# Last transform of a long convolution: four array places of 64 rows by 32 columns instead of two of 128 by 64, with the token rows ordered to match

## The chip, the cores and the metric

The kernel runs on one core of a Trainium2 chip. The metric is the device time of one execution in microseconds. A core has TensorE (PE in the profile; its weight loads are listed apart as PEld), VectorE (DVE), ScalarE (ACT), GpSimd (POOL) and SyncE (SP). SP and POOL issue DMAs here.

## The reference, cut to what matters

x is one sequence of L = 2048 tokens with D = 448 channels. Two residual steps follow each other, each with a layer norm that is scaled and shifted by vectors computed from a condition c:

```python
x = A_u
mod = (_silu(c) @ w_mod).reshape(c.shape[0], 6, 1, -1)
h = _layernorm(x, axis=-1) * (1 + ca) + sa
x = x + ga * _A_ref(h, ...)        # S4D: long convolution over tokens
h = _layernorm(x, axis=-1) * (1 + cb) + sb
x = x + gb * _B_ref(h, ...)        # mixer: MLP over tokens
...
# _A_ref: K = 2 Re sum_n C exp(A dt pos), 256 terms per channel; y = u * K (causal, by FFT of 2L) + D_skip * u
# _B_ref: h = layernorm(x); u = gelu(h^T w1 + b1) with 1792 features; y = u w2 + b2
```

## The kernel before

The convolution is a two-step Fourier transform of length 4096, written as matmuls in fp32 with small tables. A token number is split so that one step works over 32 values (n in the code), the other over 64. The channels go in two halves of 224. The program has these stages:

- Until about 384 us: the convolution's filter is generated (exponentials and sines on ACT, products on POOL and DVE, matmuls on PE), its spectrum and that of the input are made, and the first half of the channels goes through the spectral product and the inverse transform.
- 384 to 416 us: the second half of the channels. The loop over m takes 16 pairs of frequencies in steps of two. Per pair: `pc_s2` (a forward matmul into kx, line 770), `pc_mul` (DVE makes zx and zy from kx and the input's spectrum u, line 779; POOL makes the two halves of z, lines 781 and 782), `pc_inv` (the inverse matmuls into vv, line 796) and `pc_out` (ACT copies vv to vt, SP stores it into v_d in DRAM, lines 802 and 804). `pc_inv` of a step stands behind `pc_s2` of the next step. u is loaded by SP, four buffers deep (line 739). Inside this loop SP also loads the first weights of the mixer and the first tile of x.
- From 416 us: the mixer. Its first product runs over 16 groups r of 128 tokens each (r is the token number modulo 16). For each r, SP loads vt from v_d (`ln_load`), PE does the last transform of the convolution into one PSUM tile y with the table ft (`ln_y`, line 1222), DVE adds it to x (line 1225), and a layer norm, the modulation and a second layer norm follow on ACT and DVE. The result is split into a high and a low part, h3h and h3l. `mlp1` multiplies by weights that ACT and DVE have split too (whi, wlo, lines 202 and 211): 21 matmuls for each r and each half of the 1792 features, lines 1194 to 1196. PE's order is written out by hand: y of r = t + 3 stands ahead of the 21 matmuls of r = t.
- Then gelu, the second half of the features (meanwhile the new x rows are stored into x2_d, line 1310), and the second product with w2, which adds x2_d and writes the output, lines 1328 to 1334.

The rows of a tile of 128 tokens are ordered (g, n, h): 64 partitions for each g, in which n and h alternate. Rows of x, w1 and x2_d are therefore moved by two DMAs of 64 partitions. The table ft has 128 rows (32 frequencies k, real and imaginary part, and h) and 64 columns (n, h); where row and column differ in h it is zero. One y takes two matmuls, one for each g, of 128 rows by 64 columns.

The order of PE, ACT, DVE and POOL within a stage is that of the code (manual_schedule); SP's order is partly the code's (between the lines with `first` or `last`), partly a scheduler's. A weight tile is three buffers deep as loaded, four deep as split.

Of the kernel before, what the change touches and what calls it, by code (L numbers as in the profile page):

```python
# [11 lines left out]
F32 = mybir.dt.float32  # L12
# [9 lines left out]
L, D, N, F = 2048, 448, 256, 1792  # L22
P = 128
# [16 lines left out]
def dft_tables():  # L40
    n1 = np.arange(32)
    k1 = np.arange(32)
    n2 = np.arange(64)
    k2 = np.arange(64)
    nn = 4096
    t = {}
    w = 2 * np.pi * np.outer(n1, k1) / 64
    w1 = np.zeros((2, 32, 32))
    w1[0] = np.cos(w)
    w1[1] = -np.sin(w)  # L50
    w1[0, :, 0] = 1
    w1[1, :, 0] = (-1.0) ** n1
    wc = np.zeros((4, 32, 2, 4, 32))
    for g in range(4):
        for c in range(2):
            wc[g, :, c, g, :] = w1[c]
    t["WU"] = np.tile(w1.transpose(1, 2, 0).reshape(32, 64), (4, 1))

    t["WC"] = wc.reshape(P, 2, 2, 2, 32).swapaxes(3, 4).reshape(P, 2 * P)
    s = np.zeros((2, 64, 32, 2, 64))  # L60
    i1 = np.zeros((2, 64, 32, 2, 64))
    i2 = np.zeros((2, 64, 32, 2, 64))

    def inverse(rows, cols, k, m, ang):
        a = np.cos(ang) * 2 / nn
        b = np.sin(ang) * 2 / nn
        i1[0, rows, k, m[0]] = a
        i1[1, rows, k, m[0]] = -b
        i2[1, rows, k, m[0]] = -a
        i2[0, rows, k, m[0]] = -b  # L70
        if len(m) > 1:
            i1[0, rows, k, m[1]] = b
            i1[1, rows, k, m[1]] = a
            i2[1, rows, k, m[1]] = -b
            i2[0, rows, k, m[1]] = a

    for k in range(1, 32):
        ang = 2 * np.pi * np.outer(n2, k + 64 * k2) / nn
        s[0, :, k, 0] = np.cos(ang)
        s[1, :, k, 0] = np.sin(ang)  # L80
        s[0, :, k, 1] = -np.sin(ang)
        s[1, :, k, 1] = np.cos(ang)
        inverse(slice(None), None, k, (0, 1), ang.T)


    for q in range(32):
        ang = 2 * np.pi * n2 * (32 + 64 * q) / nn
        s[1, :, 0, 0, q] = np.cos(ang)
        s[1, :, 0, 1, q] = -np.sin(ang)
        inverse(q, None, 0, (1,), ang)  # L90
    for q in range(33, 64):
        ang = 2 * np.pi * n2 * (64 * (q - 32)) / nn
        s[0, :, 0, 0, q] = np.cos(ang)
        s[0, :, 0, 1, q] = -np.sin(ang)
        inverse(q, None, 0, (0,), ang)
    s[0, :, 0, 0, 32] = 1
    s[0, :, 0, 1, 32] = (-1.0) ** n2
    i1[0, 32, 0, 0] = 1 / nn
    i2[1, 32, 0, 0] = (-1.0) ** n2 / nn
    s2 = s.reshape(P, 32 * P)  # L100

    su = s.swapaxes(3, 4).reshape(2, 64, 32, P)
    t["S2"] = su.reshape(2, 4, 8, 2, 32 * P).transpose(3, 0, 2, 1, 4).reshape(P, 32 * P)

    one = np.einsum("cnk,cqkm->km", w1, su)
    t["SV"] = one[ones_k1()].T

    order = lambda a: a.reshape(P, 32, 2, 2, 2, 16).swapaxes(3, 4).reshape(2, 64, 32, P)
    v1, v2 = order(i1), order(i2)
    pairs = v1.reshape(2, 64, NP, 2, P).transpose(3, 1, 2, 0, 4).reshape(P, NP, 2 * P)  # L110
    t["SI"] = np.concatenate([s2.reshape(P, NP, 2 * P), pairs], 2).reshape(P, NP * 4 * P)
    t0 = np.zeros((P, 2, P))
    t0[32, 0] = v1[0, 32, 0] + v2[1, 32, 0]
    t0[:, 1] = pairs[:, 0, P:]
    t["T0"] = t0.reshape(P, 2 * P)
    ft = np.zeros((32, 2, 2, 32, 2))
    w = 2 * np.pi * np.outer(k1, n1) / 64
    f0 = np.cos(w)
    f1 = -np.sin(w)
    f0[0] = 1  # L120
    f1[0] = (-1.0) ** n1
    for h in range(2):
        ft[:, 0, h, :, h] = f0
        ft[:, 1, h, :, h] = f1
    t["FT"] = ft.reshape(P, 64)


    te = np.zeros((3, 64, 16, 32))
    tg = np.zeros((3, 16, 4, 16, 32))
    n = np.arange(32)  # L130
    for d in range(16):
        te[0, 2 * d : 2 * d + 2, d] = 2 * n + 1
        te[2, 2 * d : 2 * d + 2, d] = -n
        tg[0, d, 0:2, d] = n
        tg[0, d, 2:4, d] = 1
        tg[2, d, 0:2, d] = -64 * n
        tg[2, d, 2:4, d] = 1
    tg = tg.reshape(3, 16, 2, 2, 512).swapaxes(1, 2)
    tt = np.concatenate([te.reshape(3, 64, 512), tg.reshape(3, 64, 512)], 1)
    tt[1] = -tt[0]  # L140
    t["TT"] = tt.reshape(3, P, 512)
    return {k: np.ascontiguousarray(v.astype(np.float32)) for k, v in t.items()}


def ones_k1():

    return [0] + list(range(1, 32, 2))


def token_rows(a):  # L150

    return a.rearrange("(n g h r) d -> r g n h d", g=2, h=2, r=16)


def token_pair(a, r, g):

    rows = a.rearrange("(n g h r) d -> g n h (r d)", g=2, h=2, r=16)
    return rows[g, :, :, r * D : (r + 2) * D]


class WeightStream:
# [4 lines left out]
    def __init__(self, tc, ctx, i):  # L166
        self.nc = tc.nc
        self.pool = ctx.enter_context(tc.tile_pool(name="mw", bufs=WAHEAD, side="right", reuse_waits="tile"))
        self.w1 = token_rows(i["B_w1"])
        self.w2 = i["B_w2"].rearrange("(k p) s -> p k s", p=P)  # L170
        self.raw, self.parts = {}, {}
        self.loaded = self.done = 0

    def load(self):
        n = self.loaded
        if n == 64:
            return
        w = self.pool.tile([P, 896], F32, tag="w", name="w", bufs=3)
        if n < 32:
            fh, r = divmod(n, 16)  # L180
            for g in range(2):
                self.nc.sync.dma_start(w[64 * g : 64 * g + 64], self.w1[r, g, :, :, fh * 896 : (fh + 1) * 896])
        else:
            t, kh = divmod(n - 32, 2)
            self.nc.sync.dma_start(
                w.rearrange("p (k s) -> p k s", k=7), self.w2[:, 7 * kh : 7 * kh + 7, t * P : (t + 1) * P]
            )
        self.raw[n] = w
        self.loaded += 1
# [27 lines left out]
def tile_adaln_s4d_mixer(ctx, tc, i, out):  # L217
    nc = tc.nc
    x = i["A_u"][0]
# [6 lines left out]
    v_d = dram.tile([32, P, D], F32, name="v_d")  # L226
    x2_d = dram.tile([L, D], F32, name="x2_d")

    cp = ctx.enter_context(tc.tile_pool(name="cp", bufs=1))
    mod = [None] * 3 + [cp.tile([P, D], F32, name=f"mod{k}") for k in range(3, 6)]  # L230
    eps_t = cp.tile([P, 1], F32, name="eps_t")
    ft = cp.tile([P, 64], F32, name="ft")
    b1 = cp.tile([P, 14], F32, name="b1")
    b2 = cp.tile([P, 16], F32, name="b2")
    nc.vector.memset(eps_t, EPS)
# [2 lines left out]
    with ExitStack() as es:  # L238
        V, S, G, T = nc.vector, nc.scalar, nc.gpsimd, nc.tensor
# [85 lines left out]
        for q in range(4):  # L325
            r = slice(32 * q, 32 * q + 1)
# [615 lines left out]
        rows, cols, pieces = iter(range(32)), iter(range(32)), [0, 0]  # L942
# [189 lines left out]
        xts = [xs.tile([P, 2, D], F32, name=f"xt{r}") for r in range(8)]  # L1132

        def x_pair(r):
            for g in range(2):
                nc.sync.dma_start(
                    xts[r // 2][64 * g : 64 * g + 64].rearrange("p r d -> p (r d)"), token_pair(x, r, g)
                )

        swp = es.enter_context(tc.tile_pool(name="swp", bufs=2, reuse_waits="tile"))  # L1140
# [34 lines left out]
    with ExitStack() as es:  # L1175
        es.enter_context(tc.manual_schedule(engines={ENG.PE, ENG.Activation, ENG.DVE, ENG.Pool}))
        V, S, G = nc.vector, nc.scalar, nc.gpsimd
# [4 lines left out]
        h3l = kp.tile([P, 16, D], F32R, name="h3l")  # L1182
        uh = [up.tile([P, 7, D], F32R, name="uh0"), None]
        ul = [up.tile([P, 7, D], F32R, name="ul0"), None]
        v_v = v_d.rearrange("k (ch g r) d -> r (k ch) g d", ch=4, g=2)

        def mlp1(acc, n, f0=0, f1=7):
            fh, r = divmod(n, 16)
# [9 lines left out]
        vts, hs, sa, sb = {}, {}, {}, {}  # L1198

        def ln_load(r):  # L1200
            vts[r] = rot.tile([P, 2, D], F32, tag="vt", name="vt", bufs=4)
            nc.sync.dma_start(vts[r], v_v[r])
            if r % 2 and 1 < r < 15:
                x_pair(r + 1)

        def small(nm, tag):
            return rot.tile([P, 1], F32, tag=tag + nm, name=nm, bufs=3)
# [10 lines left out]
        def ln_y(r):  # L1218
            y = py.tile([P, D], F32, tag="y", name="y")
            vt = vts.pop(r)  # L1220
            for g in range(2):
                nc.tensor.matmul(y[64 * g : 64 * g + 64], ft, vt[:, g], start=True, stop=True)  # L1222
            total = small("sum", "a")
            x_ = xts[r // 2][:, r % 2]
            V.scalar_tensor_tensor(x_, x_, 1.0, y, ALU.mult, ALU.add, accum_out=total)
            return lambda: sa.update({r: stats(x_, total, "a")})
# [78 lines left out]
        acc = [pacc.tile([P, D], F32, tag="acc", name="acc") for _ in range(7)]  # L1305
        for r in range(16):
            if r < 8:
                for g in range(2):
                    rows = xts[r][64 * g : 64 * g + 64].rearrange("p r d -> p (r d)")
                    nc.sync.dma_start(token_pair(x2_d, 2 * r, g), rows)  # L1310
            wst.ahead(16 + r + WAHEAD, V)
            mlp1(acc, 16 + r)
        e2.close()
# [3 lines left out]
        for t in range(16):  # L1317
# [4 lines left out]
            for kh in range(2):  # L1322
                n = 32 + 2 * t + kh
# [7 lines left out]
            y = ru.tile([P, D], F32, tag="y", name="y")  # L1331
# [30 lines left out]
```

## Time and profile before

| | us |
|---|---|
| median of 3 runs (719.51 to 723.74) | 723.24 |
| the profiled execution | 723.32 |
| its span | 721.5 |
| PE busy in the span | 630.4 (87%) |
| DVE busy | 453.3 (63%) |
| ACT busy | 442.9 (61%) |
| POOL busy | 273.4 (38%) |
| mean granted TensorE clock | 0.924 |

Busy times are sums over records of one execution; the ends of matmuls are modelled, and a busy PE is not a PE at its peak. Lines such as L1222 are lines of the program before. A row of the timeline is: start, length, engine, line, operation, out<-in, count, and in brackets the idle time of the engine ahead of it with what ended it. Rows with SPq are DMA issues on SP's queue: the time for which the queue was taken, not the transfer.

### The profile page before, as it was taken

The page shows a single profiled execution, that of the slowest core. Times are in us where ns is not written, and L with a number is a line of the kernel's source. Part 1 is how long each engine was busy: PE and PEld are TensorE (multiplying, and loading weights), DVE is VectorE, ACT ScalarE, POOL GpSimd, SP SyncE. Part 2 cuts the span into 40 slices and gives each one's busy share as a digit, 9 for nine tenths or more (in the row PEclk, how much of TensorE's full clock was granted, in tenths as well). Part 3 has the DMA queues.
Part 4 walks back from the last instruction along what each step waited for, and adds up shares of the span by engine and source line. Part 5 has one row for each costly group of instructions (what it writes and reads, how often), then busy time and mean ns, then how long its engine had stood idle before and what let it go on. Part 6 is the DMA issues. An engine that isn't in the chain of part 4 may idle for free. (4 is left out here: it accounts for less than half of the span.)

```text
span 721.5 us, 18291 instructions
## 1 busy us (share of the span) xinstructions
PE 630.4 (87%) x7204; PEld 455.2 (63%) x7204; DVE 453.3 (63%) x875; ACT 442.9 (61%) x879; POOL 273.4 (38%) x328
## 2 busy tenths in 40 slices
PE   0659989987899888789888949999999999999997
PEld 0334334543544546556565617778999999999996
DVE  7569779769859768476785538778723263334441
ACT  5837588777988889989983549787622242222220
POOL 6487428318729788878884600000000000000000
PEclk9869857787999999989999959999999999999999
DMA  7795464356889645535236979974585436655540
GB/s 168 203 192 139 147 198 138 114 186 164 245 250 254 183 137 131 162 86 152 71 105 184 289 221 257 243 207 112 167 233 153 143 106 176 175 156 153 154 141 25
DMA packets 101636, 121.19 MB, mean 168 GB/s; under 512 B 13067, under 2 KB 87423, under 8 KB 101423
## 3 DMA queue, kind: packets, MB, share of 16 engines
q1 hardware_dynamic: 100014, 113.16, 55.3%
q0 software_dynamic: 1536, 6.87, 4.4%
q8 instruction: 57, 0.93, 0.6%
q14 instruction: 29, 0.23, 0.1%
HBM read 84.64 MB, written 34.87 MB: 166 GB/s over the span
## 5 line engine op out<-in xcount | busy, mean ns | idle before, releaser
L202 ACT CAST whi<-w 128x896 fp32r<-128x896 f32 x64 | 59.7, 938 | 131.4 <-PE o L1329 84.6
L649 POOL TENSOR_TENSOR G<-mag,gs 128x512 f32<-128x512 f32 x56 | 71.9, 1283 | 92.4 <-ACT gs L645 92.4
L211 DVE TENSOR_TENSOR wlo<-w,whi 128x896 fp32r<-128x896 f32 x64 | 68.0, 1087 | 40.3 <-ACT whi L202 27.9
L601 PE MATMUL xg<-tab,lph 64*128 64x512 f32 x112 | 68.0, 609 | 26.6 <-issue 7.9
L1194 PE MATMUL acc<-h3h,whi 128*128 128x448 f32 x224 | 83.5, 373 | 0.1
L1195 PE MATMUL acc<-h3l,whi 128*128 128x448 f32 x224 | 82.0, 366 | 0.0
L1329 PE MATMUL o<-ul,whi 128*128 128x448 f32 x224 | 81.3, 363 | 0.0
L676 PEld LDWEIGHTS kg<-E,G 128*32 128x32 f32 x3584 | 60.7, 121 | 32.5 <-issue 19.4
L1328 PE MATMUL o<-uh,whi 128*128 128x448 f32 x224 | 81.2, 362 | 0.0
L1196 PE MATMUL acc<-h3h,wlo 128*128 128x448 f32 x224 | 81.1, 362 | 0.0
L1330 PE MATMUL o<-uh,wlo 128*128 128x448 f32 x224 | 80.6, 360 | 0.0
L601 PE MATMUL xe<-tab,lph 64*128 64x512 f32 x112 | 66.7, 599 | 12.2 <-ACT gs L646 10.0
L676 PE MATMUL kg<-E,G 128*32 128x64 f32 x3584 | 70.8, 237 | 3.1 <-issue 2.3
L650 POOL TENSOR_TENSOR G<-mag,gs 128x512 f32<-128x512 f32 x56 | 71.7, 1280 | 0.0
L651 DVE TENSOR_TENSOR E<-m,xe 128x512 f32<-128x512 f32 x56 | 38.2, 683 | 39.6 <-ACT xe L644 31.5
L630 POOL TENSOR_TENSOR m<-mag,w 128x512 f32<-128x512 f32 x56 | 59.9, 1069 | 6.0 <-DVE E L655 1.5
L1332 DVE SCALAR_TENSOR_TENSOR y<-o,b,mod 128x448 f32<-128x448 f32 x16 | 10.9, 684 | 80.3 <-PE o L1330 80.3
L642 ACT ACTIVATE ab<-xe 128x512 f32<-128x512 f32 x56 | 33.6, 600 | 31.0 <-PE xe L601 18.4
L1194 PEld LDWEIGHTS acc<-h3h,whi 128*128 128x128 f32 x224 | 42.4, 189 | 13.9 <-ACT h L1250 6.3
L601 PE MATMUL xe<-tab,lex 64*128 64x512 f32 x56 | 31.2, 567 | 19.2 <-DMA lex<-wm 17.4
L601 PEld LDWEIGHTS xg<-tab,lph 64*128 64x128 f32 x112 | 24.0, 214 | 37.1 <-issue 9.8
L612 ACT ACTIVATE mag<-xe 128x512 f32<-128x512 f32 x56 | 35.5, 634 | 17.8 <-PE xg L601 11.1
(231 smaller groups left out, 1485.9 us busy)
## 6 DMA issues: line engine op xcount, KB each, us to landing
w<-in_B_w_dram SPq DMA_DIRECT2D x64, 224.0 KB
w<-in_B_w_dram SPq DMA_DIRECT2D x32, 448.0 KB
yu_d<-yt SPq DMA_DIRECT2D x16, 448.0 KB
yi<-yu_d SPq DMA_DIRECT2D x32, 224.0 KB
us_d<-uo SPq DMA_DIRECT2D x16, 448.0 KB
u<-us_d SPq DMA_DIRECT2D x32, 224.0 KB
v_d<-vt SPq DMA_DIRECT2D x32, 224.0 KB
vt<-v_d SPq DMA_DIRECT2D x16, 448.0 KB
```

Of the source, the lines that this page charges most:

```text
L211: eng.tensor_tensor(lo, w, hi.bitcast(F32), ALU.subtract)
L601: T.matmul(out[k], lhs[r], rhs[r], start=start, stop=stop)
L630: G.tensor_tensor(m2, me, w[:, :, None].to_broadcast([P, GD, 32]), ALU.mult)
L649: G.tensor_tensor(Gt[:, 1], mg_, v32(sg), ALU.mult)
L650: G.tensor_tensor(Gt[:, 0], mg_, v32(cg_), ALU.mult)
L676: T.matmul(kgs[g][32 * q : 32 * q + 32, m], Gt[:, c, d], E[:, c, d], start=h == 0 and c == 0 and m == 0, stop=h == 1 and c == 1, skip_grou ...
L1194: nc.tensor.matmul(acc[f], hi[:, fs], h3h[:, r], start=r == 0, stop=False)
L1195: nc.tensor.matmul(acc[f], hi[:, fs], h3l[:, r], start=False, stop=False)
L1196: nc.tensor.matmul(acc[f], lo[:, fs], h3h[:, r], start=False, stop=r == 15)
L1328: nc.tensor.matmul(o, hi[:, ks], uh[kh][:, k], start=kh == 0 and k == 0, stop=False)
L1329: nc.tensor.matmul(o, hi[:, ks], ul[kh][:, k], start=False, stop=False)
L1330: nc.tensor.matmul(o, lo[:, ks], uh[kh][:, k], start=False, stop=kh == 1 and k == 6)
```

## The change

The last transform of each r is done by four matmuls of 64 rows by 32 columns, one for each pair (g, h), at array rows 64 h and array columns 32 j with j = 2 g + h. The table FT loses its zeros and has 32 columns. For this the real parts, imaginary parts and frequencies of one h have to stand in one half of the partitions, so v_d is loaded by two DMAs for each r. The token rows of a tile come out in the order (g, h, n), so every load and store of token rows (w1, x, x2_d) is four DMAs of 32 partitions instead of two of 64. The loads of x, except for the first tile, are issued on POOL's queue instead of SP's. Line numbers of the mixer move by up to 3.

```diff
-    ft = np.zeros((32, 2, 2, 32, 2))
+    ft = np.zeros((2, 32, 2, 32))
...
     for h in range(2):
-        ft[:, 0, h, :, h] = f0
-        ft[:, 1, h, :, h] = f1
-    t["FT"] = ft.reshape(P, 64)
+        ft[h, :, 0] = f0
+        ft[h, :, 1] = f1
+    t["FT"] = ft.reshape(P, 32)
...
 def token_rows(a):
-    return a.rearrange("(n g h r) d -> r g n h d", g=2, h=2, r=16)
+    return a.rearrange("(n j r) d -> r j n d", j=4, r=16)
-def token_pair(a, r, g):
-    rows = a.rearrange("(n g h r) d -> g n h (r d)", g=2, h=2, r=16)
-    return rows[g, :, :, r * D : (r + 2) * D]
+def token_pair(a, r, j):
+    rows = a.rearrange("(n j r) d -> j n (r d)", j=4, r=16)
+    return rows[j, :, r * D : (r + 2) * D]
...
-            for g in range(2):
-                self.nc.sync.dma_start(w[64 * g : 64 * g + 64], self.w1[r, g, :, :, fh * 896 : (fh + 1) * 896])
+            for j in range(4):
+                self.nc.sync.dma_start(w[32 * j : 32 * j + 32], self.w1[r, j, :, fh * 896 : (fh + 1) * 896])
...
-    ft = cp.tile([P, 64], F32, name="ft")
+    ft = cp.tile([P, 32], F32, name="ft")
...
         def x_pair(r):
-            for g in range(2):
-                nc.sync.dma_start(
-                    xts[r // 2][64 * g : 64 * g + 64].rearrange("p r d -> p (r d)"), token_pair(x, r, g)
+            for j in range(4):
+                (G if r else nc.sync).dma_start(
+                    xts[r // 2][32 * j : 32 * j + 32].rearrange("p r d -> p (r d)"), token_pair(x, r, j)
                 )
...
-        v_v = v_d.rearrange("k (ch g r) d -> r (k ch) g d", ch=4, g=2)
+        v_v = v_d.rearrange("k (c h g r) d -> r h k c g d", c=2, h=2, g=2)
...
-            nc.sync.dma_start(vts[r], v_v[r])
+            for h in range(2):
+                nc.sync.dma_start(vts[r][64 * h : 64 * h + 64], v_v[r, h])
...
-            for g in range(2):
-                nc.tensor.matmul(y[64 * g : 64 * g + 64], ft, vt[:, g], start=True, stop=True)
+            for j in range(4):
+                g, h = divmod(j, 2)
+                k = slice(64 * h, 64 * h + 64)
+                nc.tensor.matmul(y[32 * j : 32 * j + 32], ft[k], vt[k, g], start=True, stop=True)
...
-                for g in range(2):
-                    rows = xts[r][64 * g : 64 * g + 64].rearrange("p r d -> p (r d)")
-                    nc.sync.dma_start(token_pair(x2_d, 2 * r, g), rows)
+                for j in range(4):
+                    rows = xts[r][32 * j : 32 * j + 32].rearrange("p r d -> p (r d)")
+                    nc.sync.dma_start(token_pair(x2_d, 2 * r, j), rows)
```

The order of instructions on PE, DVE and ACT stays the same but for y's. On POOL and SP it changes; the places are shown in the prediction.

## The prediction

> **What bounds the kernel now.** I read the granted clock and the stretches by time first, then the chain that ended last, then the timelines of PE, POOL and SP where the edited lines run. The table of stretches gives, for each stretch, the busy time of PE, of the weight loads, of DVE, ACT and POOL (instruction counts in brackets), then the granted TensorE clock, the DMA share and GB/s.
>
> ```profile
> 424.00:432.00 8.00, 5.32 (x13) 0.88 (x9) 4.17 (x14) 2.87 (x7) 0.00 (x0) 0.50 1.06 281
> ...
> 440.00:500.00 60.00, 60.00 (x285) 46.15 (x285) 47.30 (x141) 49.29 (x108) 0.00 (x0) 1.00 0.83 204
> 500.00:590.00 90.00, 90.00 (x452) 84.36 (x451) 40.62 (x65) 34.73 (x48) 0.00 (x0) 1.00 0.54 156
> ```
>
> From 440 on PE has no gap. So whatever moves the moment at which the mixer's first accumulation starts moves the end, and so does every microsecond that PE itself spends on the last transform (tile y). The chain (start, length, engine and line) shows that moment and the pace behind it.
>
> ```profile
> 413.22 2.77 DMA v_d<-vt
> ...
> 416.39 1.27 DMA v_d<-vt
> ...
> 419.55 6.80 issue
> ...
> 431.60 0.74 PE acc L1194
> ...
> 438.47 0.20 PE acc L1195
> 438.87 0.90 PE y L1222 x4
> ...
> 444.18 0.90 PE y L1222 x4
> ```
>
> The convolution's last store leaves at 416.39, the first accumulation starts at 431.60; between them lie the stores' landing, the load of vt, one transform and one layer norm. Then one r takes 444.18 - 438.87 = 5.31 us.
>
> **The transform itself.** Now 32 matmuls of 128 rows by 64 columns become 64 of 64 rows by 32 columns. Each fp32 matmul leaves two records, so one r had 4 records and gets 8. All stream 448 columns. The first three run at half clock:
>
> ```profile
> 423.64 1.76 PE L1222 MATMUL y<-vt,ft 128*64 128x448 f32 x4 [7.94 <-DMA vt<-v_d]
> 426.13 1.76 PE L1222 MATMUL y<-vt,ft 128*64 128x448 f32 x4 [0.73 <-DVE xt L1225]
> 429.72 1.76 PE L1222 MATMUL y<-vt,ft 128*64 128x448 f32 x4 [1.83 <-DVE xt L1225]
> ```
>
> Four records in 0.90 us on the chain: already two at a time, 0.45 us for each round of 448 columns. If four go at a time, 8 records are again two rounds, 0.90 us. That four can go is seen at line 714, whose 64x64 matmuls use two row halves and two column halves:
>
> ```profile
> 382.51 1.16 PE L714 MATMUL y<-wc,ks 64*64 64x64 f32 x62 [0.22 <-ACT vt L802]
> ```
>
> At y's rate a round of 64 columns takes 0.45 x 64/448 = 0.064 us; 62 records two at a time would be 31 rounds, 2.0 us; four at a time 1.0. It took 1.16. So the change buys PE nothing: what it drops is not time but the zeros in the weights. Bounds: of the 5.31 us of one r, 21 accumulating matmuls at 0.20 (as the chain's row at 438.47) are 4.2 and y 0.90, so 0.21 is the change of form and could at best go (13 r at full clock: -2.7); four more records at L714's 1.16/62 = 0.019 us are 0.07 each r (+1.0). I take 0.
>
> **x loads on POOL.** This is the costly part. Fourteen of the sixteen x loads of 64 rows leave SP's queue and become 28 loads of 32 rows on POOL's queue, and they are not issued in the mixer but between the products of the convolution's second half.
>
> POOL in the program before, at the middle of the second half (z_6187 to z_6251 are the products' outputs of four successive spectrum pairs):
>
> ```order
> L781 TENSOR_TENSOR z_6187<-zx_6185,zy_6186 128x224
> L782 TENSOR_TENSOR z_6187<-zx_6185,zy_6186 128x224
> L781 TENSOR_TENSOR z_6197<-zx_6195,zy_6196 128x224
> L782 TENSOR_TENSOR z_6197<-zx_6195,zy_6196 128x224
> L781 TENSOR_TENSOR z_6241<-zx_6239,zy_6240 128x224
> L782 TENSOR_TENSOR z_6241<-zx_6239,zy_6240 128x224
> L781 TENSOR_TENSOR z_6251<-zx_6249,zy_6250 128x224
> L782 TENSOR_TENSOR z_6251<-zx_6249,zy_6250 128x224
> ```
>
> Nothing stands between the products. POOL in the changed program, the same four pairs ( xt2 and xt3 are x tiles of the mixer):
>
> ```order
> L1136 DMA xt2_6072<-in_A_u_dram 32x896 x2
> L781 TENSOR_TENSOR z_6187<-zx_6185,zy_6186 128x224
> L782 TENSOR_TENSOR z_6187<-zx_6185,zy_6186 128x224
> L781 TENSOR_TENSOR z_6197<-zx_6195,zy_6196 128x224
> L782 TENSOR_TENSOR z_6197<-zx_6195,zy_6196 128x224
> L1136 DMA xt2_6072<-in_A_u_dram 32x896
> L1136 DMA xt3_6073<-in_A_u_dram 32x896 x2
> L781 TENSOR_TENSOR z_6241<-zx_6239,zy_6240 128x224
> L782 TENSOR_TENSOR z_6241<-zx_6239,zy_6240 128x224
> L781 TENSOR_TENSOR z_6251<-zx_6249,zy_6250 128x224
> L782 TENSOR_TENSOR z_6251<-zx_6249,zy_6250 128x224
> L1136 DMA xt3_6073<-in_A_u_dram 32x896 x2
> ```
>
> Five loads now stand among products that followed each other directly. Number the 16 pairs of the second half z16 to z31. Over all of it, 3 loads stand ahead of z16, 21 between z16 and z31, 4 behind z31. Issuing one occupies POOL, as POOL's own earlier x loads of 32 rows show:
>
> ```profile
> L292 POOL DMA_DIRECT2D xt<-in_A_u_dram x12 | 6.1, 512 | 0.0
> ```
>
> I take 0.50 us each, so 21 x 0.50 = 10.5 us. How much idle time POOL has there:
>
> ```profile
> 387.00:414.00 27.00, 25.36 (x232) 17.95 (x228) 16.93 (x31) 12.19 (x54) 19.71 (x32) 1.00 0.82 244
> ```
>
> 27.0 - 19.7 = 7.3 us. I number the gaps by the pair behind them (POOL's timeline; in brackets the idle time ahead of z18, z19, z22, z24 and z31; those ahead of z26, z28 and z30 are like z24's):
>
> ```profile
> 390.40 0.66 POOL L781 TENSOR_TENSOR z<-zx,zy 128x224 f32<-128x224 f32 x1 [0.74 <-DVE zy L779]
> ...
> 392.42 0.66 POOL L781 TENSOR_TENSOR z<-zx,zy 128x224 f32<-128x224 f32 x1 [0.74 <-DVE zy L779]
> ...
> 396.74 0.66 POOL L781 TENSOR_TENSOR z<-zx,zy 128x224 f32<-128x224 f32 x1 [0.40 <-DVE zy L779]
> ...
> 400.12 0.66 POOL L781 TENSOR_TENSOR z<-zx,zy 128x224 f32<-128x224 f32 x1 [0.85 <-DVE zy L779]
> ...
> 413.25 0.66 POOL L781 TENSOR_TENSOR z<-zx,zy 128x224 f32<-128x224 f32 x1 [1.72 <-DVE zy L779]
> ```
>
> By the new order the loads come, counted by pair: 1 ahead of z18, 1 of z19, 2 of z20, 0 of z21, 3 of z22, 0 of z23, then 2, 1, 2, 1, 2, 1, 2 ahead of z24 to z30, and 3 ahead of z31. The two of z18 and z19 fit into their gaps and leave 0.5 us of them unused. From z20 on the lag only grows: 1.0 at z20, about 1.9 at z22 and 2.0 at z24, 2.6 at z26, 3.2 at z28, 3.8 at z30, about 3.6 at z31 (its gap of 1.72 swallows more than its three loads). That agrees with the total: 10.5 - (7.3 - 0.5) = 3.7. The gaps can be filled because the consumer is one step behind: the PE reads a product only after the next step's forward matmuls, so DVE goes on feeding POOL while POOL lags. Once PE waits, PE is no longer full there (25.36 of 27 us before), and POOL is the bound. I take **+3.6 us** for the end of the convolution, between 0 (an issue so short that the gaps hold it, 7.3/21 = 0.35 us) and the transfer's own limit, below.
>
> **SP.** SP's queue at the join of the two stages in the program before (w: weights, u: the other spectrum, vt: the convolution's result, xt: x tiles):
>
> ```order
> L182 DMA w<-in_B_w_dram 64x1x896 x2
> L739 DMA u<-us_d 128x448
> L804 DMA v_d<-vt 128x2x224 x2
> L1136 DMA xt_6070<-in_A_u_dram 64x1x896 x2
> L804 DMA v_d<-vt 128x2x224 x4
> L1202 DMA vt<-v_d 128x2x448 x2
> L1136 DMA xt_6071<-in_A_u_dram 64x1x896 x2
> L1202 DMA vt<-v_d 128x2x448 x2
> ```
>
> A tile of x is asked for between the second vt and the third. The same place in the changed program:
>
> ```order
> L182 DMA w<-in_B_w_dram 32x896 x4
> L739 DMA u<-us_d 128x448
> L804 DMA v_d<-vt 128x2x224 x2
> L1136 DMA xt_6070<-in_A_u_dram 32x896 x4
> L804 DMA v_d<-vt 128x2x224 x4
> L1203 DMA vt<-v_d 64x2x448 x8
> L182 DMA w<-in_B_w_dram 32x896 x4
> ```
>
> Every w load and the first x load is four issues, every vt load two; the x loads between the vt loads are gone. The trace's issues there, and DVE's wait on the last u:
>
> ```profile
> 406.76 1.18 SPq L182 DMA_DIRECT2D w<-in_B_w_dram  x2
> 408.03 0.53 SPq L739 DMA_DIRECT2D u<-us_d  x1
> ...
> 419.71 1.23 SPq L1202 DMA_DIRECT2D vt<-v_d  x2
> ```
> ```profile
> 411.93 0.62 DVE L779 TENSOR_TENSOR zx<-kx,u 128x448 f32<-128x448 f32 x1 [1.84 <-DMA u<-us_d]
> ```
>
> The first vt took 0.6 us to issue (1.23/2) and reached PE at 423.64. Two issues of half the size cost, by the smaller DMAs of the trace, 0.3 to 0.6 each:
>
> ```profile
> L587 SPq DMA_DIRECT2D lph<-pars x27: 308/381/1691, 27.4 to 345.8; - x27
> ```
> ```profile
> L182 SPq DMA_DIRECT2D w<-in_B_w_dram x64: 528/586/1760, 383.2 to 555.5; - x64
> ```
>
> A 64-row load (w) took 0.586 at the median, a 32-row one (lph) 0.381. So the first transform's second half leaves 0 to 0.6 us later; I take **+0.5** (64 rows of v_d are nearest to w). In the same way four w issues ahead of the last u cost 1.2 to 2.3 us instead of 1.18, and u comes up to 1.1 later. That is hidden by POOL's lag of 3.6, and would be paid if that lag were not there.
>
> The four loads behind z31 put 4 x 112 KB = 0.46 MB, 1.6 us at 281 GB/s, onto the engines just ahead of the last store and the first vt: 0 to 1.6, I take **+0.4**, since the DMAs have free time there.
>
> In the mixer SP issues 6 DMAs in an r of 5.31 us, at most 3.5 us. In the second half of the first product it is 4 of w and 4 of the stored rows for eight r, 8 x 0.38 to 8 x 0.59 = 3.0 to 4.7 us against an r of 21 x 0.20 = 4.2: at most 8 x 0.5 = 4 us late. This costs nothing, since ACT's casts stand four r ahead and wait for PE, not for the load; without that lead it would be the 4 us:
>
> ```profile
> 536.00 0.94 ACT L202 CAST whi<-w 128x896 fp32r<-128x896 f32 x1 [3.26 <-PE acc L1195]
> ```
>
> The halved table FT is one smaller load long before. **Sum:** 0 + 3.6 + 0.5 + 0.4 = +4.5 us on the profiled execution's 723.32 us (span 721.5; the median of three runs is 723.24): **727.8 us**.
>
> **Rivals.** *A, the places take turns (chance 0.09).* All four matmuls of an r write the one bank of y, from two row halves; at line 714 each row half has a bank of its own, and nothing in this trace has two row halves in one bank. If they took turns, an r would have four rounds: +0.90 x 13 = 11.7, and at half clock +1.76 for the first y and +1.76 for the third, which ends just ahead of the first accumulation: +15.2, with the 4.5 above 743 us. It decides at a y group over 1.2 us. The Trainium skill, "TensorEngine Tiling (Array Packing)", Gotcha 1: PSUM Pressure, says that different row tiles cannot access the same PSUM bank at once; by that rule A is the case. I keep it low because the four write different partitions, which line 714's do not.
>
> *B, POOL's gaps hold the loads (0.17).* If an issue takes 0.35 us or less, the convolution ends as before, and without x loads beside it vt lands in 2.8 us, as the longest v_d store on the chain, instead of 423.64 - 419.71 = 3.9: 723.3 - 1.1 + 0.5 = 722.7, not slower. For it: these rows hold 3,584 bytes, those of line 292 at least 7,168 (4 x 448 x 4). Against: both are 32 rows, and the 512 ns are a mean over rows of 7,168 and 14,336 bytes.
>
> *C, the transfers are the bound (0.16).* 21 x 112 KB = 2.4 MB at 281 GB/s are 8.6 us, in a stretch with a DMA share of 0.82, that is 4.9 us free of 27. If the loads hold up u (1.84 us late already) and the stores for their full length, the end moves by 8.6 instead of 3.6: 732.8. A load also waits for the eighth before it on POOL; this joins in if a landing takes more than 8 to 9 us:
>
> ```profile
> xt<-in_A_u_dram POOLq DMA_DIRECT2D x8, 224.0 KB, 7.9
> ```
>
> **How the numbers follow.** The main case (0.58) spans 725 to 731: each load 0.45 to 0.55 us moves it by 1, PE's -2.7 to +1.0 and the tail the rest. The range takes in B and most of C and leaves A out: 721.5 to 734. A measurement of this kernel tells about 1%, 7.2 us, from no change. Over 730.5 lie A, most of C (0.14) and a little of the main case (0.04): 0.27. Below 716 only a gain that no row shows: 0.04. Between them 0.69.
>
> **What would show it.** Right: y groups of 0.9 us with 8 records; POOL near full from z20 on with DMA issues of 0.5 us; PE gaps ahead of vv in the last six steps, POOL named as releaser; the last store 3 to 5 us later; no wait of PE after the first accumulation. Wrong: y groups near 1.8 (A); z31 at its old distance from z16 (B); DVE waiting on u again and again (C); or PE waiting on weights in the mixer, which I exclude.

## The result, and the profile after

| | before | after |
|---|---|---|
| median, us (lowest to highest) | 722.80 (719.51 to 723.74), 4 runs | 731.87 (729.82 to 732.43), 4 runs |
| ratio, with its 95% interval | | 1.0154 (1.0109 to 1.0198) |
| the profiled execution, its span | 723.32, 721.5 | 729.82, 727.7 |
| mean granted clock | 0.924 | 0.926 |

The changed kernel is slower by 9.1 us between the medians and by 6.5 between the two profiled executions; the interval of the ratio is 7.9 to 14.3 us. The forecast was 727.8, with a range of 721.5 to 734; the median of 731.87 lies above the 725 to 731 of its main case.

The table of stretches of the changed kernel (columns as before: busy time of PE, weight loads, DVE, ACT and POOL, granted clock, DMA share, GB/s), with the same stretches as were shown of before:

```profile
387.00:414.00 27.00, 24.63 (x205) 14.81 (x204) 15.07 (x27) 11.90 (x53) 26.19 (x47) 1.00 1.02 296
...
440.00:500.00 60.00, 60.00 (x331) 44.92 (x324) 47.62 (x143) 49.25 (x107) 0.00 (x0) 1.00 0.64 164
500.00:590.00 90.00, 90.00 (x450) 82.50 (x449) 40.24 (x69) 36.48 (x54) 0.00 (x0) 1.00 0.54 156
```

POOL was busy for 19.71 of the first 27 us and is now for 26.19; PE fell from 25.36 to 24.63, and the DMA share rose from 0.82 to 1.02. From 440 on PE has no gap, as before.

The chain of the changed kernel from the end of the convolution into the mixer:

```profile
406.60 6.04 DMA w<-in_B_w_dram
412.71 4.65 DMA v_d<-vt
417.77 1.27 DMA v_d<-vt
...
420.92 8.96 issue
...
435.13 0.74 PE acc L1194
...
442.61 0.89 PE y L1225 x8
447.94 0.89 PE y L1225 x8
```

The eight records of a transform take 0.89 us where four took 0.90, and the pitch of an r goes from 5.31 to 447.94 - 442.61 = 5.33. A store of v_d that landed in 2.77 us now takes 4.65. (The load of w ahead of it is on the chain because SP's queue waited for its landing, for 0.5 us.)

The first two transforms, in PE's timeline of the changed kernel:

```profile
425.79 3.13 PE L1225 MATMUL y<-vt,ft 64*32 64x448 f32 x8 [8.71 <-DMA vt<-v_d]
429.66 1.72 PE L1225 MATMUL y<-vt,ft 64*32 64x448 f32 x8 [0.74 <-DVE xt L1228]
```

Both run at half clock, as before. The second takes 1.72 us (1.76 before), so the 3.13 of the first contains some 1.4 us of waiting for the second piece of its vt.

POOL's timeline of the changed kernel, at z22 and at z31 with its neighbours:

```profile
394.01 1.50 POOL L1136 DMA_DIRECT2D xt<-in_A_u_dram  x3
395.52 0.68 POOL L781 TENSOR_TENSOR z<-zx,zy 128x224 f32<-128x224 f32 x1
...
412.14 1.50 POOL L1136 DMA_DIRECT2D xt<-in_A_u_dram  x3
414.50 0.65 POOL L781 TENSOR_TENSOR z<-zx,zy 128x224 f32<-128x224 f32 x1 [0.87 <-DVE zy L779]
...
415.72 1.99 POOL L1136 DMA_DIRECT2D xt<-in_A_u_dram  x4
```

Between 389 and 413.64 POOL goes from products to loads and back without a gap: it is the bound there, at 0.50 us for each load. Only z31 waits, for DVE. DVE's waits from 384 to 420 (line, what it waited for, us in all, times, longest), first before, then after, tell which of the two causes acts when:

```profile
DVE zx L779 <- DMA u<-us_d: 1.8, 1, 1.8
DVE zx L779 <- POOL z L782: 1.2, 3, 0.5
```
```profile
DVE zx L779 <- POOL z L782: 7.0, 9, 1.6
DVE zx L779 <- DMA u<-us_d: 5.1, 2, 3.7
```

DVE's output buffers are held by the late products nine times. The last u (3.7 us of the 5.1) comes so late that zx and zy of z31 are made from it only around the time when POOL is free (413.64):

```profile
413.17 0.62 DVE L779 TENSOR_TENSOR zx<-kx,u 128x448 f32<-128x448 f32 x1 [3.75 <-DMA u<-us_d]
413.71 0.61 DVE L779 TENSOR_TENSOR zy<-kx,u 128x448 f32<-128x448 f32 x1
```

To find the time I cut each trace at five marks: the first half of z16, the first half of z31, the first issue of a vt load behind z31, the first accumulation, and the last record. All are starts in the timelines.

| kernel | z16 at | z16 to z31 | z31 to vt issue | vt issue to first acc | first acc to end | ratio to before |
|---|---|---|---|---|---|---|
| before | 387.15 | 26.10 | 6.45 | 11.89 | 289.86 | |
| after | 384.30 | 30.20 | 7.78 | 12.85 | 292.55 | 1.0154 |
| difference | -2.85 | +4.10 | +1.33 | +0.95 | +2.69 | |

The four stretches behind z16 add up to +9.07; the -2.85 ahead of it makes 6.2, the difference of the spans. That -2.85 is no gain of the change: two profiles of programs that are alike up to there differ by 6.15 us (387.15 here, 381.00 in the run e6_before_128B below). The mean granted clock shows the difference (0.89 and 0.91), first in the program before, then in that run, for the same 5562 matmuls:

```profile
0.00:387.00 387.00, 312.94 (x5562) 181.05 (x5562) 287.22 (x544) 308.25 (x615) 253.16 (x296) 0.89 0.58 164
```
```profile
0.00:381.00 381.00, 307.25 (x5562) 177.68 (x5562) 286.52 (x544) 307.68 (x615) 253.06 (x296) 0.91 0.59 167
```

So four stretches had to be explained, and the last of them, +2.69 with PE full all the way, was in no step of the prediction.

### The profile page after: what moved, and what is told of

It is laid out like the page before. It is cut to its first block, busy times and chain, and to the rows that moved or that the text cites. A ratio compares the mean times of both kernels' runs of the same rounds, so it can differ in the third digit from the quotient of the medians.

```text
span 727.7 us, 18624 instructions
## 1 busy us (share of the span) xinstructions
PE 635.6 (87%) x7268; PEld 453.5 (62%) x7268; DVE 453.8 (62%) x875; ACT 442.9 (61%) x879; POOL 286.8 (39%) x356
## 5 line engine op out<-in xcount | busy, mean ns | idle before, releaser
L676 PEld LDWEIGHTS kg<-E,G 128*32 128x32 f32 x3584 | 59.2, 119 | 29.4 <-issue 15.1
L676 PE MATMUL kg<-E,G 128*32 128x64 f32 x3584 | 69.1, 234 | 1.1 <-POOL G L649 0.5
```

What stands on the lines that cost most here:

```text
L676: T.matmul(kgs[g][32 * q : 32 * q + 32, m], Gt[:, c, d], E[:, c, d], start=h == 0 and c == 0 and m == 0, stop=h == 1 and c == 1, skip_grou ...
```

## The experiments

The kernel before ran beside each group of runs, on the same chip, so ratios are compared (0.001 is 0.72 us). The marks of all runs with their ratio and its 95% interval (e10 and e11 were executed once each, in 729.55 and 723.87 us beside 724.52 of before, which gives no ratio):

| run | z16 to z31 | z31 to vt issue | vt issue to first acc | first acc to end | ratio |
|---|---|---|---|---|---|
| e1_x_on_sp | 25.87 | 5.24 | 12.93 | 292.76 | 1.0060 (1.0030 to 1.0091) |
| e2_before_x_pool | 32.94 | 5.39 | 11.89 | 290.56 | 1.0147 (1.0107 to 1.0186) |
| e3_before_32rows | 27.57 | 5.79 | 12.51 | 289.61 | 1.0039 (1.0004 to 1.0073) |
| e4_x_late | 25.71 | 5.57 | 12.72 | 292.63 | 1.0047 (1.0010 to 1.0084) |
| e5_after_128B | 30.08 | 7.17 | 12.52 | 289.09 | 1.0079 (1.0044 to 1.0113) |
| e6_before_128B | 26.14 | 5.40 | 11.98 | 292.37 | 1.0022 (0.9986 to 1.0059) |
| e7_before_64B | 26.17 | 5.98 | 11.71 | 294.51 | 1.0048 (1.0014 to 1.0081) |
| e8_pool_small | 33.44 | 5.03 | 12.93 | 292.49 | 1.0137 (1.0081 to 1.0193) |
| e10_before_32B | 26.19 | 5.39 | 12.12 | 297.15 | |
| e11_before_192B | 26.08 | 5.06 | 11.98 | 298.01 | |
| e12_late_128B | 25.81 | 5.25 | 13.03 | 289.15 | 1.0018 (0.9987 to 1.0050) |
| e13_late_128B_vt | 25.79 | 5.24 | 12.85 | 289.82 | 1.0009 (0.9982 to 1.0037) |

**x loads back on SP**, the rest of the change kept:

```diff
-                (G if r else nc.sync).dma_start(
+                nc.sync.dma_start(
```

> The changed kernel with all x loads back on SP's queue, asked for between the vt loads as before; four places, 32-row loads and the vt load in two pieces stay. Theory P (POOL's issues delay the products, and the transfers that they start there delay u, the last store and the first vt): z16 to z31 falls from 30.2 back to 26 to 26.5 us, last product to first vt issue from 7.8 to 6.5, and the time is 723.5 to 726. Rival S (the cost is the doubled number of DMAs on SP, with the new order of rows): the time stays at 730 or more, and z31 stays late because u comes late. Rival N (some 2.7 us of the difference lie in the slower pace of PE after the first accumulation and belong to the four places): the steady pitch of the o matmuls stays at 0.202 us in place of 0.200.

z31 and the first vt come as early as in the program before, so 32-row loads on SP are not what delays them, and rival S falls. The ratio falls to 1.0060, which is 4.3 us and more than theory P allowed (0.3 to 2.8): rival N's stretch, 292.76, is untouched. So POOL's loads are not the cause of that stretch; that it belongs to the four places was N's guess and is tested below.

**The x loads of the kernel before on POOL**, 64 rows each, nothing else:

```diff
-                nc.sync.dma_start(
+                (G if r else nc.sync).dma_start(
```

> The kernel before, with its fourteen 64-row x loads behind the first pair moved to POOL and nothing else. Three stand ahead of z18, eleven between z19 and z28. If an issue costs POOL 0.5 us whatever its rows, 14 x 0.5 = 7 us nearly fit the 7.3 us of gaps, z16 to z31 is 26 to 27.5 us and the time 723 to 725. If it costs by the row (64 rows, 1.0 us), 14 us against 7.3 delay z31 by 5 to 7 and the time is 728 to 731. Rival (the bytes moved into that stretch delay u and the stores, whatever POOL does): the last store and first vt come 1 to 3 us late, with DVE named as waiting on u, and the time is 725 to 728.

This was a miss in size: with half as many issues z31 is later still, 32.94 us behind z16. POOL's timeline shows that 64 rows cost hardly more to issue than 32, and DVE's waits (384 to 420) show what took the place of the issue time:

```profile
395.15 1.59 POOL L1136 DMA_DIRECT2D xt<-in_A_u_dram  x3
```
```profile
DVE zx L779 <- DMA u<-us_d: 8.3, 4, 3.7
...
DVE zx L779 <- POOL z L782: 4.5, 6, 1.7
```

An issue takes 1.59/3 = 0.53 us (0.543 in the mean of all 14). DVE waits for u for 8.3 us in place of 1.8, and for POOL's products for 4.5 in place of 1.2. I read it as the bytes, asked for earlier than 32-row issues could ask, that delay u; issues without bytes (e8 below) leave DVE no wait for u. The rival of this run (the transfers) holds for the greater part, and costs more than it said. Moving the loads to POOL is by itself as dear as the whole change.

**DMAs of 32 rows on SP in the kernel before**, old row order (w, x, x2 in four, vt in two; the slices alone are shown):

```diff
-                    xts[r // 2][64 * g : 64 * g + 64]..., token_pair(x, r, g)
+                    xts[r // 2][32 * j : 32 * j + 32]..., token_pair(x, r, j // 2)[16 * (j % 2) : 16 * (j % 2) + 16],
...
-            nc.sync.dma_start(vts[r], v_v[r])
+            for h in range(2):
+                nc.sync.dma_start(vts[r][64 * h : 64 * h + 64], v_v[r, 64 * h : 64 * h + 64])
```

> The kernel before, with its old row order and two matmuls a transform, but each load of w and x and each store of x in four DMAs of 32 rows and each vt load in two of 64, all on SP. Theory P: only the first vt's second piece and the queue's length cost, 0.5 to 1.5 us, so 723.5 to 725; the first y waits inside itself for the second piece. Rival S (the number of DMAs on SP is what costs): 728 or more, with PE waiting on weights or DVE on u.

1.0039 is 2.8 us by the runs. In the trace it is 1.47 us at z31, -0.66 from there to the vt issue, and 0.62 behind. The -0.66 says nothing: before and the four programs that differ from it by an address alone (e6, e7, e10, e11) scatter from 5.06 to 6.45 there, and before is the highest of them. The 0.62 is not a wait between the two pieces of the first vt: its first piece is issued at 403.64, ahead of z31, and the first transform takes 1.76 us, without a wait inside it, against the expectation. It is the third transform that waits for its vt, 2.98 us, whose loads stand behind four issues of x. DVE's wait on u and that transform:

```profile
DVE zx L782 <- DMA u<-us_d: 3.3, 1, 3.3
```
```profile
429.21 1.76 PE L1227 MATMUL y<-vt,ft 128*64 128x448 f32 x4 [2.98 <-DMA vt<-v_d]
```

The last u is 1.5 us later than the 1.8 of before. The prediction put u up to 1.1 us late behind the four issues of w, and had POOL's lag hide it. But in e1 the same four issues stand ahead of u, and DVE waits 1.6 us; e3 has the early piece of vt in the queue besides. So the four issues alone are not shown to delay u. Theory P holds for the cost; S does not, since PE never waits on weights and the stretch from the first accumulation is 289.61.

**x loads on POOL, but held back to the mixer** by one-element copies:

```diff
-        def x_pair(r):
+        def x_pair(r, gate=None):
+            if gate is not None:
+                V.tensor_copy(xts[r // 2][:, 0, 0:1], gate)
...
-                x_pair(r + 1)
+                x_pair(r + 1, vts[0][:, 0, 0:1] if r == 3 else xts[(r - 4) // 2][:, 1, 0:1])
```

> The changed kernel with the x loads still on POOL, but the 24 loads behind the first pair of POOL made to wait for the mixer (one-element copies on DVE into the tile ahead of each). Theory P: z31 comes as early as before (z16 to z31 26 to 27 us, one issue in between), last product to first vt issue back near 6.5, the first vt's two pieces stay (+0.5 to +1): 723.5 to 726. Rival S: 730 or more. If the transfers only move their collision into the mixer (a vt load late), the acc stage shows it as a wait of PE, 726 to 729.

As theory P has it: 25.71 and 5.57, and PE waits for nothing from 425 us on. So the delay of z31 and the longer way to the first vt come from the place where the loads are issued, and POOL's queue does not hurt in itself. The ratio left, 1.0047, is again the pieces of vt and the last stretch.

**FT's tile at its old size** in the changed kernel, and **larger** in the kernel before. The halved table takes 128 bytes less in each partition, and every tile allocated behind it, h3h, h3l, uh and ul among them (what PE streams in the mixer), stands 128 bytes lower; the weights whi and wlo, allocated from the other end, stay.

```diff
-    ft = cp.tile([P, 32], F32, name="ft")
+    ft = cp.tile([P, 64], F32, name="ft")[:, :32]
```
```diff
-    ft = cp.tile([P, 64], F32, name="ft")
+    ft = cp.tile([P, 96], F32, name="ft")[:, :64]
```

> The changed kernel, but the tile of the halved table FT keeps its old size (64 columns, of which 32 are used), so that the tiles that lie behind it in SBUF (h3h, h3l, uh, ul) stand where they stood before; the change moved them down by 128 bytes. All programs with the smaller table so far need 292.6 us from the first accumulation to the end, all with the old one 289.6 to 290.6; in the former one matmul in three is 206.7 ns apart from the next, in the latter 201. Theory A (the address): the o pitch goes back to 0.200 us, first accumulation to end is 289.9, and the ratio to before falls from 1.0154 to about 1.0117. Rival (the four places, or the longer program of PE, slow it): pitch 0.202, 292.6 us, ratio 1.015.

> The kernel before with the tile of FT enlarged from 64 to 96 columns and used as before, which moves the tiles behind it by 128 bytes, and nothing else. Theory A: o pitch 0.202 us, first accumulation to end 292.6, ratio 1.0037. Rival: pitch 0.200, 289.9 us, ratio 1.000.

The second diff is e6; e7, e10 and e11 have 80, 72 and 112 in place of 96.

> The kernel before with the tile of FT enlarged to 80 columns: the tiles behind it move by 64 bytes. Theory A leaves open what this place gives: a pitch between 0.197 (the shortest of the three seen) and 0.2067 us for each of the three matmuls, so first accumulation to end between 286 and 299 us. Rival: 289.9 us as before.

> The kernel before with the tile of FT enlarged to 72 columns: the tiles behind it (h3h, h3l, uh, ul) move by 32 bytes, to an address of 64 in each 256. So far 32 of 256 gave a pitch of 0.200 us, 96 gave 0.204, 160 gave 0.202. If the pitch follows the place within 256 bytes smoothly it is 0.201 to 0.203 here, first accumulation to end 291 to 294 us; if it follows the distance to the weight tiles (all at 224 of 256), nothing says which, and 286 to 299 is open.

> The kernel before with the tile of FT enlarged to 112 columns: the tiles behind it move by 192 bytes, to 224 of 256, where the weight tiles stand too. If reads of the two from like addresses disturb each other, the pitch is above 0.204 us and first accumulation to end above 294 us; if the place alone counts it can also be the shortest, down to 286 us.

Theory A (the address; it is not rival A of the prediction) holds in both directions by the last stretch: 289.09 in e5, 292.37 in e6. The ratios alone would not show it: e6's interval takes in 1, and e5's 1.0079 is below the 1.0117 that was expected. The row of the table of stretches from 600 to 700 us, where PE has no gap and the granted clock is 1.00, counts the matmuls. Before, after, e5 and e6, in this order:

```profile
600.00:700.00 100.00, 100.00 (x502) 93.73 (x501) 39.01 (x48) 21.89 (x24) 0.00 (x0) 1.00 0.58 161
```
```profile
600.00:700.00 100.00, 100.00 (x497) 92.70 (x496) 38.67 (x47) 22.56 (x24) 0.00 (x0) 1.00 0.58 161
```
```profile
600.00:700.00 100.00, 100.00 (x501) 93.73 (x501) 38.96 (x48) 22.66 (x24) 0.00 (x0) 1.00 0.57 161
```
```profile
600.00:700.00 100.00, 100.00 (x496) 92.71 (x495) 39.74 (x48) 21.73 (x23) 0.00 (x0) 1.00 0.53 152
```

The same instructions come at 502 or 501 in 100 us with the old address and at 497 or 496 with the moved one, whatever the transform's form. The two other shifts of which an extreme was expected, e10 (32 bytes) and e11 (192 bytes):

```profile
600.00:700.00 100.00, 100.00 (x488) 91.40 (x488) 39.24 (x48) 21.68 (x23) 0.00 (x0) 1.00 0.56 157
```
```profile
600.00:700.00 100.00, 100.00 (x485) 90.84 (x484) 36.44 (x44) 21.85 (x24) 0.00 (x0) 1.00 0.55 156
```

In the builds h3h, h3l, uh and ul all have the same place in 256 bytes. By that place the mean pitch of the second product's matmuls (start to start) is 200.0 ns at 32 (before), 205.3 at 64 (e10), 204.0 at 96 (e7), 202.2 at 160 and 206.7 at 224 (e11). The changed kernel and e6, both at 160, stand 256 bytes apart and agree. That is not smooth, so the first reading of e10's expectation (201 to 203) missed. At 224, where the weight tiles stand too, it is slowest, as the first reading of e11 had it; why is open, since moving the weight tiles was not tried. The place of before is the best of the five.

**POOL's issues without the bytes**: x on SP, and 28 loads of 8 bytes a row on POOL that nothing reads.

```diff
-                (G if r else nc.sync).dma_start(
+                nc.sync.dma_start(
                     xts[r // 2][32 * j : 32 * j + 32].rearrange("p r d -> p (r d)"), token_pair(x, r, j)
                 )
+                if r:
+                    G.dma_start(xq[r // 2][32 * j : 32 * j + 32], token_pair(x, r, j)[:, :2])
```

> The changed kernel with the x loads on SP and 28 extra loads of 32 rows by 2 elements on POOL into scratch tiles that nothing reads: POOL's issues almost without bytes. Seven stand ahead of z17, 21 between z17 and z26. Theory I (the issue time on POOL delays the products): 21 x 0.5 = 10.5 us against gaps of 3.9 up to z26 and 3.4 behind it, so z31 comes about 3 us late (z16 to z31 29 us) and the time is 726 to 728 on the scale of 723.2 before. Theory T (the bytes that the loads move delay u and the stores): z16 to z31 26 us and a time like that of the run with x on SP, ratio 1.006.

Theory I holds, and the size was too small: 33.44, 7.3 us later than before. The group of these loads, DVE's waits, and z31 in POOL's timeline:

```profile
L1141 POOL DMA_DIRECT2D xq<-in_A_u_dram x28 | 14.0, 505 | 0.0
```
```profile
DVE zx L779 <- POOL z L782: 9.8, 8, 3.0
```
```profile
420.61 0.66 POOL L781 TENSOR_TENSOR z<-zx,zy 128x224 f32<-128x224 f32 x1 [2.48 <-DVE zy L779]
```

505 ns for 0.2 KB, 506 for 112 KB in the changed kernel: the issue does not depend on the bytes. DVE no longer waits on u at all. By z26 the 21 issues are 10.5 us against gaps of some 4, a lag of 6.6, and the gaps behind z26 were to take back half of it. They did not: z31 has even a gap of 2.48 us. From 384 to 424 us PE waits for POOL's products seven times, 6.9 us in all, against once and 1.4 us before. My reading is that once PE has waited for a product, the forward matmuls that feed DVE are late too, and the gaps come back behind the lag.

**Both causes taken away at once**, e4 with FT's tile at its old size; and the same with the second pieces of the first four vt loads on ACT's queue:

> The changed kernel with both suspected causes taken away at once: the 24 x loads on POOL held back to the mixer, and FT's tile at its old size so that the tiles behind it keep their addresses. If the two add up, z16 to z31 is 25.7 to 26.1 us, first accumulation to end 289 to 290, and only the vt load in two pieces is left, +0.6 to +1.0 us from the vt issue to the first accumulation: ratio 1.000 to 1.003 where the changed kernel has 1.0154. If something else in the change costs, the ratio stays at 1.005 or more.

```diff
-                nc.sync.dma_start(vts[r][64 * h : 64 * h + 64], v_v[r, h])
+                (S if h and r < 4 else nc.sync).dma_start(vts[r][64 * h : 64 * h + 64], v_v[r, h])
```

> As the run above, with the second pieces of the first four vt loads issued by ACT beside SP's first pieces, so that an r's two pieces leave together. If the second piece's issue is what makes the first transform late, vt issue to first accumulation falls from 12.5 to 12.9 us to 11.9 or less (the one-piece load has 11.9; four half-size issues in place of eight ahead of the third vt can gain 1 more), and the ratio is 0.997 to 1.001. If the landing of the pieces and not their issue is late, it stays at 12.5 to 12.9 and the ratio at that of the run above.

With both gone the ratio is 1.0018, as expected, and all stretches but one are those of before. The other edit did not shorten that one: 12.85 us. Its issues, on SP's and ACT's queue, and the first transform:

```profile
417.10 3.14 SPq L1205 DMA_DIRECT2D vt<-v_d  x4
...
417.11 0.65 ACTq L1205 DMA_DIRECT2D vt<-v_d  x1
...
420.93 2.85 PE L1227 MATMUL y<-vt,ft 64*32 64x448 f32 x8 [6.70 <-DMA vt<-v_d]
```

Both pieces leave at the same time, and the second is still 2.85 - 1.72 = 1.1 us behind the first at PE. So it is their landing that is late and not the issue; why the second lands later is not shown. 1.0009 can't be told from 1.000 or from the run above: with all that costs taken out but the pieces of vt, the four places bring nothing that these runs can measure, and none of these versions beats the kernel before.

## Why the prediction was half right

The time fell into the range, but into the region over 730.5, to which the prediction gave 0.27. The range reached that far because it took in most of rival C, and C's mechanism is not what happened: that the range held is partly luck.

- **The transform itself, 0:** right. A group takes 0.89 us with eight records, so the places run four at a time, and rival A (743 us) falls. The Trainium skill, "TensorEngine Tiling (Array Packing)", Gotcha 1: PSUM Pressure, says that different row tiles cannot access the same PSUM bank at once. By this trace two row halves that write different partitions of one bank do not take turns.
- **POOL's lag, +3.6:** right in place, price and size: 506 ns for each load, no gap from z20 on, z31 4.10 us late. Of that 3.24 is POOL's. The other 0.86 is u: POOL was free at 413.64 and waited for zy until 414.50, where the prediction had hidden u behind POOL's lag. The argument that gaps swallow the loads held for z18 and z19; e8 shows that it fails once PE waits. Rival B needed issues of 0.35 us. The Trainium skill, "DMA: Bandwidth & Descriptors", Anatomy of one DMA — SWDGE (gpsimd) path, calls descriptor generation small; here one issue takes POOL, the engine that makes the products, 0.50 us, and the trace does not tell how much of it is descriptor generation.
- **Loads behind z31, +0.4:** too small. The way from z31 to the first vt is 1.33 us longer in the profiled pair, and 7.17 to 7.78 us in the two runs with these loads there against 5.03 to 6.45 in all others. As before has the highest of those, the loads may cost more than 1.33. Most of it is the landing of the last store. SP's wait for it, before and after, and what the stores meet from 416 to 420 us, in the same order:

```profile
SPq L1202 <- DMA v_d<-vt: 2.8, 1, 2.8
```
```profile
SPq L1203 <- DMA v_d<-vt: 4.0, 1, 4.0
```
```profile
416.00:420.00 4.00, 0.00 (x0) 0.00 (x0) 1.32 (x3) 3.52 (x6) 0.00 (x0) 0.50 0.20 67
```
```profile
416.00:420.00 4.00, 1.07 (x6) 0.46 (x4) 0.06 (x1) 2.83 (x6) 1.70 (x4) 0.50 1.06 341
```

  The wait is 3.8 us in e5, which has these loads there too, and 1.7 to 2.8 in all other runs. "The DMAs have free time there" was read off before (a share of 0.20); the change fills it (1.06).
- **vt in two pieces, +0.5:** 0.95. The runs with two pieces behind z31 have 12.52 to 13.03 us from issue to first accumulation, those with one 11.71 to 12.12. The mechanism was put down to the second issue; e13 shows the landing.
- **The step that failed:** "The halved table FT is one smaller load long before". It was costed as a load, at nothing, and its place in memory was not looked at. Its tile is also 128 bytes smaller, and that moves what PE streams for the rest of the program: +2.69 us from the first accumulation on, shown by undoing it (e5) and by doing it alone (e6). Why the address sets the pace stays open. The statement that PE would not wait there was right, and so the loss could not appear as a wait.
- **Rival C, 732.8:** the time is near, the mechanism is not: the transfers do not bound the stretch of the changed kernel up to 413.64. They do for the greater part in e2, where fewer issues ask for the same bytes earlier. By that run, loading faster on POOL would not have helped.

The terms as measured, 0 + 4.10 + 1.33 + 0.95 + 2.69 = 9.07, come to the 9.1 between the medians. To a tenth that is luck, as the terms are from one profile each and the ratio's interval is 7.9 to 14.3 us. Of the 4.6 by which the sum of 4.5 fell short of 9.07, 2.7 are the address.

## What to carry to other kernels

A DMA issued by an engine that also makes products costs that engine its issue time, here 0.50 to 0.55 us from 0.2 to 224 KB, and in e8 the lag was not given back by gaps further on once the consumer had waited; hold such loads back until the engine is free (e4). When a tile changes its size, look at which tiles move in SBUF, and compare the count of matmuls in a stretch where PE has no gap: a changed pace shows in no wait. Two half loads that the first consumer needs together were both there later than one whole load, even when they left together (e13).

## What the runs showed of the hardware that was not expected

- A 128x128 by 448 matmul's pitch at granted clock 1.00 depended on where in 256 bytes the streamed operand stood: 200.0 to 206.7 ns at the five places tried, 3.3%, up to 8.15 us of this kernel (298.01 - 289.86). At 160 in 256 the loss falls on one matmul of three: in the changed kernel uh with whi is followed 206.7 ns later, the two others 199.1 and 200.9; at 64, 96 and 224 all three are slow.
- An issue on POOL took 0.505 us for 32 rows of 8 bytes, 0.506 for 32 rows of 3,584 bytes and 0.543 for 64 rows of 3,584 bytes (means of 28, 28 and 14).
- The five programs alike up to z16 (before, e6, e7, e10, e11) reached it between 380.57 and 387.15 us; the two ends of the pair shown above differ in granted clock, 0.91 and 0.89. A difference of 1% between two profiles has to be cut by stages before it says anything.
